# Sliding-window attention into a gated block on one core: two identity matrices built by VectorE from index tables, and three attention groups placed on other units

## The chip, the cores and the metric

The kernel runs on one core of a Trainium2 chip. The metric is the device time in microseconds (us) of one execution, taken as the median of several runs. A profile, taken by the hardware profiler in one further execution, gives the start and the length of each instruction on each engine. TensorE (PE in the profile) does the matmuls, with its weight loads shown apart as PEld; VectorE is DVE, ScalarE is ACT, GpSimd is POOL, and SyncE is SP. SP, ACT and POOL also issue the DMA transfers.

## The reference, cut to what matters

```python
# attention: batch 4, 8 heads, 768 positions, head size 64, 4 sink positions, window 128
scores = q @ k.T / 8
keep = (column < 4) | ((row - column >= 0) & (row - column < 128))
a = softmax(where(keep, scores, -1e9))
x = (a @ v), heads side by side      # 3072 tokens x 512
# gated block
g = x @ w_gate                       # 512 -> 1536
out = (g * sigmoid(g) * (x @ w_val)) @ w_out   # 1536 -> 512
```

Each query sees at most 128 keys behind it and the first four positions ("sinks").

## The kernel before, in words

**Groups and blocks.** The attention is cut into 12 groups of 256 tokens (three to a batch), each with two tiles `j` of 128 queries. The gated block is cut into eight token blocks (`SIZES`, line 43) of 256, 256, 256, 512, 512, 512, 512 and 256 tokens. The attention of later groups is woven by hand into the matmuls of the block, so that TensorE has work while the other engines do the softmax.

**The steps of a group `g`.** `T(g)` is two steps (line 533): each turns the keys and queries of half of the heads on TensorE with 64-wide matmuls against an identity (line 260) and has ACT and DVE copy them out (line 266); the second one also issues the loads of group `g+2` (`next_load`). Groups 0 to 3 take this way; groups 4 to 11 are turned by DMA transposes on SP (`C(g)`, line 304). `Ss(g)` is two steps of scores (line 333), each with four PSUM banks, an exponential per head on ACT (line 339) and a mask multiply on DVE (line 344). `K(g)` computes the scores against the sinks (lines 362 and 366). `PVs(g)` is four steps, one for each half of the heads `hh` and each tile `j`, in the order (0,0), (1,0) with the first half, then (0,1), (1,1) written as (j,hh): matmuls into one bank `o` (line 388), then on DVE a reciprocal (393) and a multiply into `xn` (400), which frees the bank. For group 3 and for groups 5 and up the second half of a tile ends with a DMA transpose of `xn` into `xT` on SP (line 406); the other groups turn `xn` on TensorE (`step_X`, 424).

**The block.** `gate` (436) projects a block of tokens: matmuls into `pg`, a tanh `th` on ACT (459), then any attention steps, then matmuls into `pv` (452), then on DVE `u` (466) and `ht` (467), which free `pg` and `pv`. `down` (494) multiplies the 12 pieces of `ht` with `w_out` (506), spreading its attention steps between them; ACT copies the result out (510) and SP writes it (512).

**Order.** Each engine runs its instructions in the order in which they were written. `weave` (556) walks a list of units (one `gate` or `down` call each), and `slots` says which attention steps are inside which unit. DVE work of a step is put into `later` and written out at the next `flush`: at the end of the unit's own products in a `gate`, after each step in a `down`. The first such list (652) has units 0 to 24; units 15 to 20 are the gates of block 2, unit 21 and 22 the downs of block 1, units 23 and 24 the downs of block 2. In the trace the `pg` matmuls of units 18, 19 and 20 start at 57.35, 59.47 and 61.58 us, and unit 21 at 64.49 us. After it comes block 3, which needs `xT` of groups 3 and 4. For block 5 (line 675) the units 0 to 11 are its gates.

**PSUM.** There are eight banks. A new tile takes the bank that comes free first in the written order, so the scores of a unit take the banks that older `o`, `pg` and `pv` tiles leave.

**The start.** DVE clears the identities `ident` and `id32`, the tile `wm` and others. TensorE runs eight matmuls on `wm` (245). POOL issues two loads of `kq` (167), then writes the diagonals of the two identities with an affine select each (`make_identity`), then two index tables `tq` and `tk` with iota (179 and 181), then the loads of `va`, of group 1, and of the weights. `build_masks` (217) has DVE compare `tq` and `tk` into the masks.

Of the kernel before, what the change touches and what calls it, by code (L numbers as in the profile page):

```python
# [7 lines left out]

FP32 = mybir.dt.float32
# [2 lines left out]
ALU = mybir.AluOpType  # L12
# [3 lines left out]
def kernel(  # L16
# [12 lines left out]
    nc = tc.nc  # L29
# [115 lines left out]
    ident = const.tile([P, P], BF16)  # L145
# [3 lines left out]
    tq = const.tile([P, P], FP32)  # L149
    tk = const.tile([P, 1], FP32)  # L150
# [4 lines left out]
        ks = const.tile([P, NP2 * KS], BF16, tag=f"ks{b}", name="ks")  # L155
        kss.append(ks)

    nc.vector.memset(ident, 0.0)
    wm = const.tile([P, 512], BF16)
    nc.vector.memset(wm, 0.0)  # L160
    wake = const.tile([P, 1], FP32)
# [10 lines left out]
            st[64:P], four_tokens(q, 0, slice(2 * p, 2 * p + 2)))  # L172
        first.append(st)
    id32 = const.tile([P, P], FP32)
    nc.vector.memset(id32, 0.0)
    make_identity(nc, ident, nomemset=True)
    make_identity(nc, id32, nomemset=True)

    nc.gpsimd.iota(tq, [[1, P]], base=0, channel_multiplier=0,
                   allow_small_or_imprecise_dtypes=True)  # L180
# [35 lines left out]

    def build_masks():

        tq2 = tq.rearrange("p (o x) -> p o x", o=1).broadcast_to([P, 2, P])
        nc.vector.tensor_scalar(mask[:, :, P:2 * P], tq2, tk, None, op0=ALU.is_ge)  # L220

        nc.vector.tensor_scalar(sk, tk, float(NS), None, op0=ALU.is_lt)
        flat, flat0 = (m.rearrange("p a x -> p (a x)") for m in (mask, mask0))
        nc.vector.tensor_scalar(mask[:, :, 0:P], tq2, tk, None, op0=ALU.is_lt)
        nc.vector.tensor_scalar(
            flat0[:, P:3 * P], flat[:, P:3 * P], sk, None, op0=ALU.max)
        nc.vector.tensor_copy(out=flat0[:, 3 * P:4 * P], in_=flat[:, 3 * P:4 * P])
# [5 lines left out]
    def A(fn, *a):  # L233
        return lambda: fn(*a)
# [35 lines left out]
    def step_T(g, ph, which=(0, 1), q_copy=None, q_late=False):  # L270

        if g not in kTs:
            new_kq(g)
        evict = turn(g, (2 * ph, 2 * ph + 1), which,
                     lambda i, p: nat[g][:, 2 * p:2 * p + 2], (ident, ident))
        if 0 in which:
            evict(0, nc.scalar.copy)
        if 1 in which:
            q = A(evict, 1, q_copy or nc.vector.tensor_copy)
            if q_late:  # L280
                later.append(q)
            else:
                q()
# [16 lines left out]
    def cross_T(g):  # L300

        t = crossp.tile([P, 2, 2, NP2, P], BF16, tag="kqT", name="kqT")
        for j in range(2):
            nc.sync.dma_start(
                t[:, j].rearrange("q i a m -> q (i a) m"),
                nat[g][:, j].rearrange("p i x -> p (i x)"), transpose=True)
        cross[g] = t
# [211 lines left out]
    def gates(tb):  # L519
        return [(gate, tb, f) for f in range(0, DFC, 512 // SIZES[tb])]  # L520

    def downs(tb):
        return [(down, tb, t) for t in range(SIZES[tb] // P)]

    def next_load(g):
        if g + 2 < NG:
            load1(g + 2)
            load_v(g + 2)

    def sinks(b):  # L530
        return [lambda: later.append(A(step_ks, b))]

    def T(g):
        def last():
            step_T(g, 1)
            next_load(g)
        return [A(step_T, g, 0), last]

    def Ss(g):
        return [A(step_S, g, p, p + 1) for p in (0, 2)]  # L540

    def PVs(g):

        return [A(step_PV, g, j, hh) for hh in range(2) for j in range(2)]

    def Xs(g):
        return [A(step_X, g, j) for j in range(2)]

    def K(g):
        return A(step_K, g)  # L550
# [5 lines left out]
    def weave(us, slots):  # L556
        assert all(i < len(us) for i in slots)
        for i, (fn, tb, x) in enumerate(us):
            fn(tb, x, slots.get(i, []))
# [7 lines left out]
    def slots(*pairs):  # L567
        sl = {}
        for at, steps in pairs:
            for i, step in zip(at if isinstance(at, tuple) else (at,) * len(steps),  # L570
                               steps):
                sl.setdefault(i, []).append(step)
        return sl

    def C(g):

        def last():
            cross_T(g)
            next_load(g)
        return [last]  # L580
# [4 lines left out]
    def first_T(p):  # L585
# [5 lines left out]
        evict(1, nc.vector.tensor_copy)  # L591

    build_masks()
    first_T(0)
    first_T(1)
# [47 lines left out]
    def first_PVs():  # L643
# [10 lines left out]
    weave(us, slots(  # L654
        (0, [flush, K(1), A(step_S, 1, 2, 3)]), (2, [first_PVs]),
        (3, [A(step_X, 1, 0), A(step_X, 1, 1, True), flush]),
        (9, T(2)), ((10, 11), Ss(2)), (10, [K(2)]),
        (12, PVs(2)[:2] + [flush]), (13, PVs(2)[2:] + [flush]), (13, C(4)),
        (14, [A(step_X, 2, 0), A(step_X, 2, 1, True), flush]),
        (15, T(3)), ((16, 17), Ss(3)), (17, sinks(1)), ((18, 18, 19, 19), PVs(3)), (19, [flush]),  # L660
        (18, C(5)), ((20, 21), Ss(4)), (21, [K(4)]),
        ((22, 22, 23, 23), PVs(4)), (24, Xs(4))))

    def pair(ga, gb, sh=0):
        s = sh
        return [((s, s + 2), Ss(ga)), ((s + 4, s + 5, s + 6, s + 7), PVs(ga)),
                ((s + 6, s + 8), Ss(gb)),
                ((10, 10, 11, 11) if s else (10, 11, 12, 13), PVs(gb))]
# [4 lines left out]
        (0, sinks(2)), *pair(7, 8), (3, [K(7)]),  # L673
        (4, C(9)), (11, C(10)), (14, C(11))))
    weave(gates(5) + downs(5), slots(
        (0, sinks(3)), *pair(9, 10), (6, [K(10)])))
    weave(gates(6) + gates(7) + downs(6) + downs(7), slots(
        ((0, 2), Ss(11)), ((4, 5, 6, 7), PVs(11))))

# [34 lines left out]
```

## Time and profile before

| what | value |
|---|---|
| median of 5 runs | 241.24 us (241.21, 242.59, 243.25, 241.24, 240.88) |
| the profiled execution | 241.21 us, its span 239.5 us |
| PE busy | 233.5 us, 98% of the span |
| DVE busy | 159.1 us, 66% |
| ACT busy | 113.2 us, 47% |
| POOL busy | 70.9 us, 30% |
| PE busy from 0 to 25 us | 22.42 of 25.00 |
| PE busy from 25 to 60 us | 35.00 of 35.00 |
| PE busy from 60 to 66 us | 5.78 of 6.00 |
| PE busy from 66 to 161 us | 95.00 of 95.00 |
| PE busy from 161 to 167 us | 5.83 of 6.00 |
| PE busy from 167 to 235 us | 68.00 of 68.00 |

The span is the time from the first to the last instruction of the profile; 1.7 us of the execution lie around it. "Busy" on PE includes time in which a matmul's pipeline drains, so a small wait of TensorE shows less in the busy time than in the distance between the starts of two groups of matmuls. The timeline of an engine has the start, the length, the operation and, in square brackets, the idle time before it with what ended it.

### The profile page before, as it was taken

The numbers are of one execution on the slowest core, as the hardware profiler recorded it, in microseconds if no ns is written. First come the engines' busy times: TensorE is split into PE (matmuls) and PEld (weight loads), VectorE is DVE, ScalarE is ACT, GpSimd is POOL, SyncE is SP. The second block draws the span as 40 slices with busy tenths as digits, with TensorE's granted clock in tenths as the row PEclk, the third lists the DMA queues.
The fourth block names the chain that finished last, engine by engine and source line by source line (L and its number), as shares of the span: only waits on it lengthen the run. The fifth ranks groups of instructions, "written<-read, shape, count | busy, mean of one in ns | idle before, by whom it ended". The sixth has DMA issues, their size and how long they took to land.

```text
span 239.5 us, 5227 instructions
## 1 busy us (share of the span) xinstructions
PE 233.5 (98%) x2083; PEld 135.8 (57%) x2083; DVE 159.1 (66%) x337; ACT 113.2 (47%) x230; POOL 70.9 (30%) x92
## 2 busy tenths in 40 slices
PE   7899999999999999999999999999999999999994
PEld 3578887678645445444445454444454445488444
DVE  4679788849963698970698961598971499877100
ACT  2888347248551764512755611556611662232112
POOL 8986387409817079000808000000000000000000
PEclk9999999999999999999999999999999999999999
DMA  7999999999999999918999936600204200200132
GB/s 140 162 183 197 204 190 204 167 208 116 151 165 164 213 162 143 114 22 206 128 154 85 146 67 170 127 0 4 44 0 131 90 0 3 44 0 3 45 131 88
DMA packets 98936, 27.37 MB, mean 114 GB/s; under 512 B 84832, under 2 KB 95968, under 8 KB 98912
## 3 DMA queue, kind: packets, MB, share of 16 engines
q0 software_dynamic: 68832, 13.90, 68.7%
q1 hardware_dynamic: 29504, 12.69, 24.8%
q10 hardware_dynamic: 576, 0.46, 0.6%
q8 instruction: 16, 0.26, 0.4%
q14 instruction: 8, 0.07, 0.1%
HBM read 28.34 MB, written 6.29 MB: 145 GB/s over the span
## 4 chain that ended last, share of the span: by engine, by line
PE 90%; ACT 4%; DVE 4%; issue 1%; DVEq 0%
PE pv L452 25%; PE pd L506 25%; PE pg L452 24%; PE o L388 5%; PE s L333 4%; ACT e L339 3%; PE pt L260 3%; PE wm L245 2%; DVE xn L400 1%; PE pd L487 1%; PE px L424 1%; DVE e L344 1%; ACT xn L396 1%; DVE u L466 1%; DVE rcp L393 0%
## 5 line engine op out<-in xcount | busy, mean ns | idle before, releaser
L452 PE MATMUL pv<-xT,wv 128*128 128x256 bf16 (+1 forms) x384 | 74.4, 326 | 0.3 <-DVE xn L400 0.3
L452 PE MATMUL pg<-xT,wg 128*128 128x256 bf16 (+1 forms) x384 | 74.2, 326 | 0.0
L459 ACT ACTIVATE th<-pg 128x512 f32<-128x512 f32 x72 | 43.8, 608 | 60.2 <-PE pg L452 59.7
L466 DVE SCALAR_TENSOR_TENSOR u<-th,pg 128x512 bf16<-128x512 f32 x72 | 49.1, 682 | 30.9 <-ACT th L459 30.2
L506 PE MATMUL pd<-wo,ht 128*128 128x512 bf16 x276 | 63.2, 379 | 0.0
L467 DVE TENSOR_TENSOR ht<-u,pv 128x512 bf16<-128x512 bf16 x72 | 49.5, 688 | 10.1 <-PE pv L452 3.2
L452 PEld LDWEIGHTS <-wg 128*128 128x128 bf16 x384 | 37.4, 98 | 25.4 <-issue 0.2
L339 ACT ACTIVATE e<-s 128x512 bf16<-128x512 f32 (+1 forms) x96 | 46.3, 581 | 1.6 <-PE s L333 1.3
L452 PEld LDWEIGHTS <-wv 128*128 128x128 bf16 x384 | 34.1, 98 | 20.6 <-issue 2.9
L506 PEld LDWEIGHTS <-ht 128*128 128x128 bf16 x276 | 26.0, 98 | 28.4 <-issue 0.2
L510 ACT ACTIVATE ot<-pd 128x512 f32<-128x512 f32 x23 | 13.7, 597 | 52.6 <-PE pd L506 50.2
L344 DVE TENSOR_TENSOR e<-e,mask 128x1024 bf16<-128x1024 bf16 (+2 forms) x49 | 29.1, 630 | 1.8 <-ACT e L339 1.7
L107 POOL DMA_DIRECT2D kq<-in_k_dram x16 | 14.4, 902 | 49.9 <-DMA kqT<-kq 49.1
L123 POOL DMA_DIRECT2D va<-in_v_dram x24 | 21.6, 920 | 2.1 <-DMA kq<-in_q_dram 0.7
L388 PEld LDWEIGHTS <-e 128*128 128x128 bf16 x352 | 16.3, 98 | 6.2 <-DVE e L344 0.9
L400 DVE TENSOR_TENSOR xn<-o,rcp 128x256 bf16<-128x256 f32 x44 | 18.7, 424 | 1.8 <-DMA xT<-xn 0.3
L388 PE MATMUL o<-va,e 128*128 128x65 bf16 x352 | 17.9, 193 | 0.3 <-DVE e L344 0.2
L107 POOL DMA_DIRECT2D kq<-in_q_dram x16 | 14.6, 911 | 1.1 <-DMA wo<-in_moe_w_out_dram 1.1
L393 DVE RECIPROCAL rcp<-o 128x4 f32<-128x4 f32 x48 | 8.3, 175 | 7.5 <-PE o L388 7.5
L491 DVE TENSOR_SCALAR ot<-pd 128x128 f32<-128x128 f32 x1 | 0.3, 292 | 14.4 <-PE pd L487 14.4
L333 PE MATMUL s<-kqT 64*128 64x128 bf16 (+1 forms) x168 | 9.4, 238 | 0.0
L388 PE MATMUL o<-vsb,es 128*128 128x260 bf16 x32 | 8.8, 274 | 0.0
(61 smaller groups left out, 107.5 us busy)
## 6 DMA issues: line engine op xcount, KB each, us to landing
out_dram<-ot SPq DMA_DIRECT2D x23, 256.0 KB
va<-in_v_dram POOLq DMA_DIRECT2D x24, 128.0 KB, 6.4
kq<-in_k_dram POOLq DMA_DIRECT2D x18, 128.0 KB, 4.4
kq<-in_q_dram POOLq DMA_DIRECT2D x16, 128.0 KB, 5.0
wo<-in_moe_w_out_dram POOLq DMA_DIRECT2D x4, 384.0 KB, 12.7
wg<-in_moe_w_gate_dram POOLq DMA_DIRECT2D x4, 256.0 KB, 8.0
wv<-in_moe_w_val_dram POOLq DMA_DIRECT2D x4, 256.0 KB, 8.5
kq<-in_k_dram POOLq DMA_DIRECT2D x3, 256.0 KB, 8.8
```

Source lines behind the costliest of these rows:

```text
L107: nc.gpsimd.dma_start(x[:, j, i].rearrange("p (h d) -> p h d", d=D), src[b, :, t0:t0 + P].rearrange("h m d -> m h d"))
L123: nc.gpsimd.dma_start(va[:, j, :, 0:D], v[b, :, t0:t0 + P].rearrange("h m d -> m h d"))
L333: nc.tensor.matmul(pss[2 * i + h][:, col:col + n * P], keys(b, t, r, p), queries(g, r, p, j, n), start=True, stop=True)
L339: nc.scalar.activation(e_t[g][:, 2 * p + h, lo:512], pss[2 * i + h][:, lo:512], AF.Exp, scale=scale)
L344: nc.vector.tensor_tensor(e, e, m[:, :, lo:512].broadcast_to([P, e.shape[1], 512 - lo]), op=ALU.mult)
L388: nc.tensor.matmul(o, l, r, start=(i == 0), stop=(i == len(mms) - 1), skip_group_check=True)
L400: nc.vector.tensor_tensor(xns[g, j][:, 256 * hh:256 * (hh + 1)].rearrange("p (h d) -> p h d", h=4), po[:, :, 0:D], rcp.broadcast_to([P, 4, ...
L452: nc.tensor.matmul(ps[:, i * n:(i + 1) * n], ws[fi][:, c, fo * P:(fo + 1) * P], x[:, 0:n // P, c], start=(c == 0), stop=(c == DMC - 1))
L459: nc.scalar.activation(th, pg, AF.Tanh, scale=0.5)
L466: nc.vector.scalar_tensor_tensor(u, th, 1.0, pg, op0=ALU.add, op1=ALU.mult)
L467: nc.vector.tensor_tensor(hts[tb][:, f:f + two].rearrange("p a n -> p (a n)"), u, pv, op=ALU.mult)
L506: nc.tensor.matmul(po, hts[tb][:, f, ts * P:(ts + 1) * P], wos[f // n][:, f % n], start=(f == 0), stop=(f == DFC - 1))
```

## The change

The two identities are no longer cleared by DVE and filled by POOL. DVE builds them in `build_masks`, ahead of the masks, by comparing the index tables for equality. POOL's affine selects are gone, so that its iota instructions and the loads behind them follow directly on the first two loads.

In the first list of units, the second `T(2)` step moves from unit 9 to unit 10, and `K(2)` from unit 10 to unit 11. The four `PVs(3)` steps, before two in unit 18 and two in unit 19 with a `flush`, are now one in each of the units 18, 19, 21 and 22. In block 5, `K(10)` moves from unit 6 to unit 5.

The line numbers in the text are those of the kernel before; in the changed kernel they are up to five lower.

```diff
-from concourse.masks import make_identity
...
-    nc.vector.memset(ident, 0.0)
...
-    nc.vector.memset(id32, 0.0)
-    make_identity(nc, ident, nomemset=True)
-    make_identity(nc, id32, nomemset=True)
...
     def build_masks():
+        for t in (ident, id32):
+            nc.vector.tensor_scalar(t, tq, tk, None, op0=ALU.is_equal)
         tq2 = tq.rearrange("p (o x) -> p o x", o=1).broadcast_to([P, 2, P])
...
-        (9, T(2)), ((10, 11), Ss(2)), (10, [K(2)]),
+        ((9, 10), T(2)), (11, [K(2)]), ((10, 11), Ss(2)),
...
-        (15, T(3)), ((16, 17), Ss(3)), (17, sinks(1)), ((18, 18, 19, 19), PVs(3)), (19, [flush]),
-        (18, C(5)), ((20, 21), Ss(4)), (21, [K(4)]),
+        (15, T(3)), ((16, 17), Ss(3)), (17, sinks(1)), ((18, 19), PVs(3)[:2]),
+        (18, C(5)), ((20, 21), Ss(4)), (21, [K(4)]), ((21, 22), PVs(3)[2:]),
...
-        (0, sinks(3)), *pair(9, 10), (6, [K(10)])))
+        (0, sinks(3)), *pair(9, 10), (5, [K(10)])))
```

## The prediction

> **What bounds the kernel now.** I read the page's busy times and chain first, then who waited for whom on PE, then the busy time by stretch, and last the timelines around the few places where PE waits.
>
> ```profile
> PE 233.5 (98%) x2083; PEld 135.8 (57%) x2083; DVE 159.1 (66%) x337; ACT 113.2 (47%) x230; POOL 70.9 (30%) x92
> PE 90%; ACT 4%; DVE 4%; issue 1%; DVEq 0%
> ```
>
> PE is the bound: nine tenths of the chain are its own work. Only PE's waits can be won, and they lie in three places, as the stretches in the table show: 0 to 25 us, around 63 us and around 164 us. Elsewhere PE is busy without a break.
>
> The second place, in the chain of waits:
>
> ```profile
> 60.50 0.14 PE o L388 x4
> ...
> 62.58 0.42 DVE xn L400
> ...
> 63.13 0.43 DVE xn L400
> ...
> 63.61 1.05 PE pv L452 x8
> ```
>
> Four `xn` multiplies of group 3 run one behind another on DVE (at 61.48, 62.03, 62.58 and 63.13), and PE's `pv` of unit 20 waits for the last. PE's timeline, here and at the third place:
>
> ```profile
> 61.58 1.04 PE L452 MATMUL pg<-xT,wg 128*128 128x256 bf16 x8
> 62.55 0.23 PE L333 MATMUL s<-kqT,kT 64*128 64x128 bf16 x2
> ...
> 63.61 1.05 PE L452 MATMUL pv<-xT,wv 128*128 128x256 bf16 x8 [0.16 <-DVE xn L400]
> ```
>
> ```profile
> 163.41 0.62 PE L333 MATMUL s<-kqT 64*128 64x128 bf16 x12
> 164.04 0.40 PE L362 MATMUL pk<-kqT,ks 128*32 128x256 bf16 x8
> 164.59 1.04 PE L452 MATMUL pv<-xT,wv 128*128 128x512 bf16 x4 [0.15 <-DVE xn L400]
> ```
>
> The twelve score matmuls from 62.55 to 63.61 take 1.06 us; the same twelve take 0.55 in unit 21 (65.45 to 66.00). The banks they ask for are those of group 3's `o` tiles.
>
> The start, on POOL and on DVE:
>
> ```profile
> 2.76 0.33 POOL masks.py:199 TENSOR_SCALAR_AFFINE_SELECT ident<-ident 128x128 bf16<-128x128 bf16 x1
> ...
> 3.26 0.27 POOL L179 IOTA tq<- 128x128 f32 x1
> 3.45 0.16 POOL L181 IOTA tk<- 128x1 f32 x1
> 3.53 1.84 POOL L123 DMA_DIRECT2D va<-in_v_dram  x2
> ```
>
> ```profile
> 3.64 0.35 DVE L220 TENSOR_SCALAR mask<-tq,tk 128x256 bf16<-128x256 f32 x1 [1.50 <-POOL tk L181]
> ...
> 4.80 0.58 DVE L227 COPY mask<-mask 128x128 bf16<-128x128 bf16 x1
> 6.18 0.42 DVE L266 CAST qT<-pt 128x256 bf16<-128x256 f32 x1 [0.80 <-PE pt L260]
> ```
>
> PE does not use the identities before its first transposes at 4.91 us, and these wait for the first `kq` load (the weight loads sat idle 0.89 us until it landed), not for POOL.
>
> **The change part by part.**
>
> *Group 3 spread.* In units 18 and 19 DVE now has one `xn` pair each in place of two. A pair (reciprocal and multiply) takes 0.55 us by the distance of the rows above. Following DVE's order: `ht` of unit 18 ends at 61.27 as before, the first pair at 61.82, `u` and `ht` of unit 19 at 63.2, the second pair at 63.75, `u` of unit 20 at 64.43. Units 18 and 19 had 24 `o` matmuls and now have 12, which is 0.36 us less work before unit 20 (twelve take 0.36, from 58.23 to 58.59), so PE wants the score banks from 62.55 − 0.36 = 62.2. They are now those of unit 17's `pv`, unit 18's `pg` and `pv`, and the first `o`: the last is free at 61.82. `pv` takes unit 19's `pg`, free after its `u` at 62.5, and is wanted at 62.75. No wait is left: 1.06 − 0.55 = **0.51 us** gained. The 0.36 of `o` matmuls come back in units 21 and 22. What is late next: the second scores of group 4 in unit 21 take the second `o` bank (free 63.75) and unit 20's `pg` (free 64.43), wanted at 64.3 and 64.5 (unit 21 starts at 64.49 − 0.51 − 0.36 = 63.62, its first three `pd` matmuls take 0.65, and the third bank is wanted 0.23 after the first). This fits by 0.07 only, so I charge 0.07 for it. Bounds of the part: 0.51, and 0, if the wait is only handed on to these two.
>
> *What the moved steps carry.* Each tile's second half ends in an SP transpose of `xn`. Before they were issued at 68.65, behind the two `kqT` transposes of group 5, which held SP from 64.69 to 68.54. Now the first `xn` is whole at about 68.2 (DVE has the group-4 masks first, 66.24 to 68.73 before, some 0.5 sooner now), so the first transpose still goes at about 68.65. The second stands behind the first (1.2 us) and unit 21's output (0.5 us): about 70.5 instead of 69.9. DVE's fourth `xn` of group 4's first half waited for the first transpose until 71.17 before, so one took 2.5 us to be read; the second would be in place by 73. Block 3 asks for it at 77.70 − 0.51 = 77.2. The cover is 4 us, so I cost it at nothing.
>
> *K(10) to unit 5.* From 163.41 to 164.59 PE takes 1.18 us for scores and `pk`. Scores take 0.55; four `pk` matmuls take 0.23 (37.60 to 37.83), so eight 0.45: 1.00 in all, and **0.18 us** are waits for DVE. With `pk` in unit 5, the `pv` of unit 6 takes the bank of unit 5's `pv`, whose `ht` ended at 163.99 before, and wants it at about 164.4 (163.41 + 0.45 + 0.55). The ACT exponential of `pk` moves from 165.79 into ACT's idle 1.37 us before 163.39. Bounds: 0.18 and 0.
>
> *Group 2 spread.* The same instructions, one unit apart. PE waits nowhere between 25 and 60 us, so nothing can be won. ACT's exponential of the sinks comes before the second scores' ones in unit 11 instead of after the first, which puts the last of those about 0.4 us later; their masks end about 43.5, and the PE step that needs them starts at 44.00. Cover 0.5 us: cost nothing. The loads of group 4 are issued at 37.88 behind others, after the moved transposes end (about 37.1), so they do not move. Bounds: 0, and −0.4 if that cover fails.
>
> *Identities.* DVE loses two clears (0.11 and 0.17 us) and gains two compares of 128 columns. None is in the trace: half of the 0.35 of the 256-column compare gives 0.18, the 0.58 of the 128-column copy is the other end. I take 0.2 each, nearest to the same operation. POOL drops 0.5 us (2.76 to 3.26), so `tk` is there at 3.1, the identities at 3.5, needed at 4.9. The masks end at 5.4 − 0.5 + 0.4 = 5.3, or 6.1 at the dear end; DVE's next work is at 6.18. Cost nothing either way.
>
> *Loads 0.5 us sooner.* In the PE rows above 25 us no wait ends in a weight or `va` load; the chain there runs over ACT exponentials, DVE and PE. From 16.57 on POOL itself waits for landings before it may issue (0.37, 0.59, 0.61 us and so on), so its lead turns into waiting. Value 0; bounds 0 and 0.5 gained. The first warm-up matmul may start 0.11 sooner, but the transposes behind it wait for the `kq` load: 0.
>
> [...]
>
> **The sum.** 0.51 + 0.18 less 0.07 for the tight place in unit 21 = 0.62. The profiled execution took 241.21 us, its span 239.5 and 1.7 around it; it stands 0.03 below the median. 241.21 − 0.62 = 240.6.
>
> **Rivals.**
>
> *The wait is handed on.* DVE is nearly full from 60 to 66 us (5.55 of 6.00) and no DVE work goes away, so the banks could be late elsewhere. Against it: DVE sat idle 0.76, 0.58, 1.19 and 0.57 us at 69 to 74, just where the moved pairs go. Time: 241.2 with nothing gained.
>
> *The loads count after all.* For it: gate weights land 7.3 to 10.6 us after issue, and the first, issued at 6.71, is used at 15.60, which leaves little. Then the full 0.5 comes on top: 241.21 − 0.51 − 0.18 − 0.5 = 240.0.
>
> *The late transpose of group 3 makes block 3 wait (slower).* If the second `xT` lands after 77.2, PE waits for each us beyond. Issued at 70.5 it decides from 6.7 us on. The nearest transpose took 2.5, but other transfers of this kernel took 5.0 (median of `kq`), 9.1 (`wv`) and up to 13.4. At 9.1 it would land at 79.6: 2.4 lost, 0.6 gained, 243.0.
>
> **How the numbers follow.** Forecast 0.60; handed on 0.18; loads 0.10; late transpose 0.07; the rest, a start that shifts by more than I see, 0.05. Low end: 240.0 less 0.3, which is how far the fastest run lies below the profiled one: 239.7. High end: nothing gained (241.2), 0.2 lost by the masks and 0.3 of scatter: 241.7. The late transpose stays outside. About 1% (2.4 us) is what a measurement of this kernel can tell from no change; the sum is a quarter of it. Faster by over 1% needs four times the sum: 0.04. Slower by over 1% needs a transpose later than 9 us or so: 0.06. Within 1%: 0.90.
>
> **What would show it.** Right: scores of unit 20 take 0.55 us; no `xn` in the chain around 63 us; `pv` follows `pk` at 162 without a wait; PE without idle time elsewhere after 25 us; the start before 25 us unchanged within 0.3 us although `va` is issued at about 3.0. Wrong: PE idle before block 3 at 77 us with `xT` as its releaser; identities over 0.6 us each; a new `xn` or `ht` wait in units 21 to 23; first transposes later than 5 us.

## The result

The changed kernel took 240.32 us (median of 41 runs, 239.73 to 241.97), the kernel before 241.06 us (78 runs): a ratio of 0.9967, 95% interval 0.9957 to 0.9977. That is 0.74 us less, by the interval 0.55 to 1.04. The forecast was 240.6 us, 0.62 under the profiled execution of the kernel before (241.21). The ratios, and the medians of the experiments, leave out executions far above the others of their kernel; the one in the profile of group 3 moved one unit too far is such a one (granted clock 0.986 in the mean), so its waits are read and its span is not.

The profiled execution of the changed kernel took 240.12 us, its span 238.4 us, 1.1 less than before. The page's busy times and the chain's shares by engine:

```profile
PE 232.8 (98%) x2083; PEld 135.5 (57%) x2083; DVE 159.1 (67%) x337; ACT 113.4 (48%) x230; POOL 70.4 (30%) x90
PE 91%; ACT 3%; DMA 2%; DVE 1%; issue 0%; POOL 0%; DVEq 0%; POOLq 0%
```

PE still bounds the kernel. DVE has the same work, POOL two instructions fewer, and a share of DMA has come into the chain, where there was none:

```profile
2.05 5.35 DMA kq<-in_k_dram
```

This is the second `kq` load of group 0. It is not among the loads that the change moves: both kernels issue it at 2.05 us, and it landed at 7.40 in place of 6.74. Over all 14 profiles it landed at 6.65 to 7.55 us (mean 7.17) in the six with early loads and at 6.74 to 7.12 (mean 6.89) in the eight others, so the loads issued sooner behind it may hold it up; no run tests that. Around 63 us the chain now reads (start, length, what):

```profile
60.90 0.87 PE pg L450 x8
61.78 0.55 PE s L331 x12
62.33 0.98 PE pv L450 x8
63.30 0.65 PE pd L504 x3
63.95 0.65 PE s L331 x12
```

No `o` and no `xn` stands between the pieces of PE any more. The twelve scores of unit 20 take 0.55 us in place of 1.06. Those of unit 21 take 0.65 in place of 0.55: the tight place that the prediction charged with 0.07. PE is busy for 6.00 of the 6.00 us from 60 to 66, and again from 161 to 167. The third place in PE's timeline:

```profile
162.96 0.62 PE L331 MATMUL s<-kqT 64*128 64x128 bf16 x12
163.51 1.04 PE L450 MATMUL pv<-xT,wv 128*128 128x512 bf16 x4
```

`pv` follows the scores after 0.55 us without a wait. The start, on POOL and on DVE:

```profile
2.76 0.28 POOL L174 IOTA tq<- 128x128 f32 x1
2.95 0.17 POOL L176 IOTA tk<- 128x1 f32 x1
3.03 1.91 POOL L122 DMA_DIRECT2D va<-in_v_dram  x2
```

```profile
3.16 0.29 DVE L216 TENSOR_SCALAR ident<-tq,tk 128x128 bf16<-128x128 f32 x1 [1.23 <-POOL tk L176]
3.36 0.65 DVE L216 TENSOR_SCALAR id<-tq,tk 128x128 f32<-128x128 f32 x1
...
4.70 0.30 DVE L225 COPY mask<-mask 128x128 bf16<-128x128 bf16 x1
5.85 0.89 DVE L264 CAST qT<-pt 128x256 bf16<-128x256 f32 x2 [0.84 <-PE pt L258]
```

The loads are issued 0.5 us sooner, and DVE is through with identities and masks at 5.0 us, long before its next work.

Where the 1.1 us of the span came from is read from the starts of groups of matmuls, which show waits that the busy time doesn't: PE's busy time from 60 to 66 us rose by 0.22, while the scores of unit 20 got 0.51 shorter. Each stretch lies between the first `pg` matmuls of two units or blocks, and the last one ends at the first `pd` of block 5's downs:

| stretch | before | after | difference |
|---|---|---|---|
| start to unit 0 | 15.60 | 15.00 | -0.60 |
| unit 0 to unit 9 | 17.62 | 17.62 | 0 |
| unit 9 to unit 12 (group 2) | 7.89 | 8.02 | +0.13 |
| unit 12 to unit 18 | 16.24 | 16.24 | 0 |
| unit 18 to block 3 (group 3) | 20.35 | 19.93 | -0.42 |
| block 3 to the downs of block 5 (K(10)) | 98.00 | 97.81 | -0.19 |

The three moved groups make -0.48 together, the start -0.60. That start is more than the forecast allowed (0.3), one of its signs of being right that did not come, so it is the main question of the experiments.

### The profile page after: what moved, and what is told of

Read it like the earlier page. It is cut to its first block, busy times and chain, and to the rows that moved or that the text cites. A ratio compares the mean times of both kernels' runs of the same rounds, so it can differ in the third digit from the quotient of the medians.

```text
span 238.4 us, 5224 instructions
## 1 busy us (share of the span) xinstructions
PE 232.8 (98%) x2083; PEld 135.5 (57%) x2083; DVE 159.1 (67%) x337; ACT 113.4 (48%) x230; POOL 70.4 (30%) x90
## 4 chain that ended last, share of the span: by engine, by line
PE 91%; ACT 3%; DMA 2%; DVE 1%; issue 0%; POOL 0%; DVEq 0%; POOLq 0%
PE pv L450 26%; PE pg L450 25%; PE pd L504 25%; PE o L386 5%; PE s L331 5%; DMA kq<-in_k_dram 2%; PE pt L258 2%; ACT e L337 2%; PE pd L485 1%; PE px L422 1%; DVE e L342 1%; ACT xn L394 1%; PE pk L360 1%; POOL kq L165 0%; ACT th L457 0%
```

## The experiments

Theory: the moved groups 3 and 10 give the gain, and the start of the profile taken after the change is not owed to the change. First rival: the earlier loads give a part of it. Second rival: the margin in front of block 3 is about to be used up. Ratios are to runs of the kernel before in the same job (a batch of runs on one chip), with 95% intervals; "start" is the first `pg` of unit 0 in the run's profile. A ratio on record is not just that of the two medians and lies up to 0.0025 off it: for "after, again" the medians give 0.9964. The kernel before has medians of 241.12, 240.99 and 241.16 us in the three jobs.

| kernel | median, us | ratio | start | 9 to 12 | 18 to block 3 | block 3 to downs 5 |
|---|---|---|---|---|---|---|
| identities alone | 240.88 | 1.0001 (0.9973 to 1.0029) | 15.03 | 7.94 | 20.15 | 97.99 |
| group 3 alone | 240.90 | 0.9982 (0.9962 to 1.0002) | 14.76 | 7.89 | 19.84 | 97.99 |
| K(10) alone | 240.86 | 0.9978 (0.9958 to 0.9998) | 14.81 | 8.10 | 20.21 | 97.80 |
| group 2 alone | 241.41 | 1.0021 (0.9995 to 1.0047) | 15.73 | 8.02 | 20.16 | 98.48 |
| before, again | 241.24 | 1.0007 (0.9989 to 1.0025) | 15.53 | 8.02 | 20.48 | 98.43 |
| after, group 2 back | 240.44 | 0.9977 (0.9960 to 0.9994) | 15.08 | 7.89 | 19.91 | 97.81 |
| after, loads 0.5 later | 240.57 | 0.9985 (0.9966 to 1.0004) | 15.46 | 8.02 | 20.03 | 97.81 |
| after, group 3 too late | 243.69 | 1.0116 (1.0084 to 1.0149) | 15.01 | 8.02 | 23.94 | not read |
| after, loads 1.5 later | 241.50 | 1.0004 (0.9976 to 1.0033) | 15.61 | 8.02 | 19.91 | 97.81 |
| groups alone | 240.83 | 0.9982 (0.9951 to 1.0012) | 14.74 | 8.57 | 20.04 | 97.80 |
| after, again | 240.29 | 0.9939 (0.9915 to 0.9964) | 15.56 | 8.02 | 19.84 | 97.80 |
| after, mended | 240.29 | 0.9945 (0.9924 to 0.9967) | 15.39 | 7.89 | 19.84 | 97.80 |

The first four and the next four rows are a job each, and the last four are one.

**One part alone.** Each kernel is the one before with one part of the diff shown above.

Identities:

> The kernel before with the identities built by VectorE and nothing else. If the start's 0.6 us in the profiled pair only came from the moment at which TensorE's matmuls become fast, this kernel equals the kernel before: 0.0 us (within 0.3), and its own profile may show either length of the first transposes. If the earlier loads or the shorter work of GpSimd bring it, it is 0.3 to 0.6 us faster, in this kernel's median too.

Group 3:

> The kernel before with only the four PV steps of group 3 spread over units 18, 19, 21 and 22. My theory: scores of unit 20 take 0.55 instead of 1.06 us, the scores of unit 21 lose 0.07 to 0.1, so 0.40 to 0.45 us faster. Rival (the wait is handed on): the chain shows DVE's xn or u in units 21 to 23 and the time is unchanged.

K(10):

> The kernel before with only K(10) moved from unit 6 to unit 5 of block 5. My theory: 0.18 us faster, with pv of unit 6 directly behind the scores. Rival: 0.0, the wait reappears one unit on.

Group 2:

> The kernel before with only the second T(2) step and K(2) one unit later. By the prediction 0.0 us. By the profile of the changed kernel 0.1 us slower, since two runs of 32 transposes take 0.57 us each where 64 in one run take 1.02.

Group 3 and K(10) shorten their own stretches and no other. Without K(10)'s move the last stretch takes 97.99 to 98.48, with it 97.80 or 97.81. Group 3's varies more: 20.15 to 20.48 without the move (five profiles, mean 20.27), 19.84 to 20.04 with it (eight, mean 19.92). The ratios point the same way; group 3's interval reaches 1 and K(10)'s just misses it. K(10)'s ratio would be 0.5 us, more than its stretch shows, so the sizes are taken from the stretches. Identities alone: not resolved. Group 2 alone did not come out at nothing: its stretch is 0.13 us longer than that of the kernel before. PE's timeline of the kernel before, and of the changed one, has the cause:

```profile
34.18 1.09 PE L260 MATMUL pt<-ident,kq 64*64 64x64 bf16 x64
35.20 1.05 PE L452 MATMUL pv<-xT,wv 128*128 128x256 bf16 x8
```

```profile
33.59 0.64 PE L258 MATMUL pt<-ident,kq 64*64 64x64 bf16 x32
34.16 1.05 PE L450 MATMUL pv<-xT,wv 128*128 128x256 bf16 x8
```

64 transposes in one run hold PE for 1.02 us (34.18 to 35.20), 32 for 0.57. Two runs of 32 are 1.14.

**The kernel before, once more, as a control.**

> The kernel before, unchanged, as a measure of the measurement: ratio 1.000 within its interval. Its profile shows where the transposes of the first two head pairs end. If TensorE's speed-up comes at a moment that the kernel does not set, this may differ by up to 1 us from the 6.99 us of the first profile; if the kernel sets it, it is 6.9 to 7.1 again.

The ratio's interval holds 1. In its profile the first scores start at 6.31 us, in the first profile of the same kernel at 6.92: the kernel does not set that moment.

**The changed kernel with group 2 as before.**

```diff
-        ((9, 10), T(2)), (11, [K(2)]), ((10, 11), Ss(2)),
+        (9, T(2)), ((10, 11), Ss(2)), (10, [K(2)]),
```

> The changed kernel with group 2 put back. If the split of the transposes costs 0.1 us, this is 0.1 faster than the changed kernel, about 0.85 faster than the kernel before; if group 2's spread helps, it is slower than the changed kernel.

Its stretch is back at 7.89. The 0.13 us don't show in the medians, which scatter by more.

**What sets the start.** In every profile TensorE's first transposes begin at 4.9 to 5.2 us. The timelines of PE at 5.8 us, of the kernel before and of the changed one:

```profile
5.89 0.31 PE L260 MATMUL pt<-ident,kq 64*64 64x64 bf16 x1
```

```profile
5.84 0.24 PE L258 MATMUL pt<-ident,kq 64*64 64x64 bf16 x1
```

The same matmul takes 0.31 us in the one and 0.24 in the other. Before, the transposes stay at 0.31 until the first scores at 6.92; after, they drop to 0.24 at 5.25, and the scores start at 6.32: 0.60 us sooner, which is the whole gain of the start. The granted clock reads 1.00 in both, so that row doesn't show it. It isn't the change either: with the identities as before (K(10) alone, group 3 alone) they are quick from 5.0 on, in four of six such profiles and in five of eight with the identities by DVE, and the changed kernel once more is slow until 6.4 and starts at 15.56:

> The changed kernel once more, as the measure for the other three. Ratio 0.997, 0.3 to 0.8 us under the kernel before. Its profile shows a first pg at 15.0 if TensorE gets quick before the first transposes end, and at about 15.5 if later: if the start of the profile taken after the change was owed to the change, 15.0 again; if it was owed to when TensorE gets quick, either.

That profile has the same start as that of the kernel before (15.56 and 15.60), and the two executions differ by 0.65 us (240.56 and 241.21), of which the stretches give 0.62: -0.51 (group 3), -0.20 (K(10)), +0.13 (group 2), -0.04 (start). Other matmuls change their pace too: the first ones on `wm` start 0.43 us apart, those of the same shape at 10.5 us in the kernel before 0.21 (the small transposes gain less, 0.31 to 0.24 in length). The moment moves: of the 14 profiles, nine have quick transposes from 4.9 to 5.7 us on, one of them (identities alone) quick matmuls from about 4.0, and five have quick ones only after 6.3, so it moves by more than 2 us. No run here shows what sets it. The seven earliest starts (14.74 to 15.08) all have quick transposes by 5.71 us, but that isn't enough: the control (15.53) and the mended kernel below (15.39) have them from 5.0 on and start late, since PE waited for loads (0.6 us in the one, 0.5 and 0.2 in the other).

**Do the loads count?** Here the changed kernel got two affine selects on tiles that nobody reads ahead of the index tables, with DVE's two clears, or six behind them:

```diff
+    nc.vector.memset(spare, 0.0)
+    nc.vector.memset(spare32, 0.0)
+    make_identity(nc, spare, nomemset=True)
+    make_identity(nc, spare32, nomemset=True)
```

> The changed kernel with GpSimd's two affine selects (and VectorE's two clears) put back on spare tiles that nobody reads, so that the loads are issued 0.5 us later, as before. If the earlier loads do nothing, the time is that of the changed kernel, 0.7 to 0.8 us under the kernel before. If they bring 0.3 or more, this is 0.3 slower than the changed kernel.

> The changed kernel with six more affine selects of POOL on tiles that nobody reads, behind the iotas, and two clears of these by DVE: the va loads and all behind them are issued about 1.5 us later than in the changed kernel, 1.0 later than in the kernel before. If the time of the loads doesn't matter up to there: within 0.2 us of the changed kernel in the same job, no PE wait on a DMA over 0.3 us before 26 us. If the loads bind when TensorE's start is quick: a PE wait on a DMA landing of 0.5 to 1.5 us before 26 us, and 0.5 to 1.0 us more than the changed kernel. If each 0.5 us is handed on in full: 1.5 us more, ratio about 1.003.

And the three groups alone, with the identities by GpSimd:

> The kernel before with groups 2, 3 and 10 moved, its identities as they were. If the identities and the earlier loads give nothing: the same time as the changed kernel, 0.46 us under the kernel before by the three sums from the profiles (0.40 and 0.19 gained, 0.13 lost), ratio 0.998. If they give something: 0.3 us or more above the changed kernel in the same job, ratio 0.999 or more. From the first pg of unit 9 to that of unit 12: 8.02 us; K(10) stretch 25.0; unit 18 to block 3 19.94.

In the last job the groups alone took 240.83 us and the changed kernel 240.29; eight of the twelve runs of the first lie above the slowest of the second (240.56). The difference of the medians is 0.54 us, by resampling the runs 0.13 to 1.32. With the loads 1.5 us later than in the changed kernel it is 1.21 us (0.76 to 1.94). So in this job the loads count, against the forecast. In the job before, the kernel with loads 0.5 us late stood 0.13 us (-0.25 to 0.33) over the one with group 2 back, and group 2 makes 0.13 of difference between these two by itself: there nothing is left for the loads. Identities alone, which has the loads 0.5 us sooner too, lay 0.25 us under the kernel before by the medians and level with it by the ratio. The loads' landings say that the lead lasts on the average: the second `kq` of group 2 landed at 32.97 to 33.64 us (mean 33.30) in the six profiles with early loads, at 33.07 to 34.22 (mean 33.77) in the seven with loads as before or put back to there. The two ranges overlap, so in a single pair of executions the lead can be gone.

The 1.21 us need not be the loads' alone. Beside POOL's six selects DVE took twice as long for the f32 identity (1.28 us in place of 0.65):

```profile
3.38 1.28 DVE L224 TENSOR_SCALAR id<-tq,tk 128x128 f32<-128x128 f32 x1
```

The masks ended at 6.38 in place of 5.0, and the first `qT` copy, which starts at 5.7 to 6.1 where the transposes are quick, had to stand behind them (6.32).

The profile of the groups alone shows how the loads get into the chain (its first part, in order of time):

```profile
2.76 0.32 POOL ident masks.py:199
3.08 0.24 POOL id masks.py:199
...
3.60 1.75 POOL va L123 x2
5.36 1.37 POOL kq L96 x2
...
10.23 9.55 DMA va<-in_v_dram
19.78 0.04 issue
19.82 0.39 PE o L388 x7
...
21.00 13.21 DMA kq<-in_q_dram
```

PE's start was early in this execution (14.74). So the chain runs not over PE, ACT and DVE, as before, but over POOL: the two affine selects, 0.56 us, stand in it, then all issues down to `va` of group 1, whose landing PE waits for, and on to `kq` of group 2. PE's list of waits:

```profile
PE o L388 <- DMA va<-in_v_dram: 0.6, 2, 0.4
PE pt L260 <- DMA kq<-in_q_dram: 0.3, 1, 0.3
```

From unit 0 to 9 this execution took 17.99 us, and from 9 to 12 8.57, in place of 17.62 and 8.02: 0.92 us lost, more than the early start had won. An early start with loads as late doesn't always pay so: group 3 alone started at 14.76 and lost nothing (17.63 and 7.89), its two `va` having landed 8.9 us after issue, by the median, and not 9.4. The changed kernel (15.00) kept its 17.62 and 8.02. The control lost in the same way: quick transposes, then 0.61 us of waiting at 13.5 us for the second `kq` of group 1. The profile with loads 1.5 us late started late itself (15.61) and shows no wait on a load over 0.3 us; that its median is 1.2 us worse is measured, but not how it divides between the loads and the late masks.

**The margin before block 3.** The second halves of group 3 one unit further on:

```diff
-        (18, C(5)), ((20, 21), Ss(4)), (21, [K(4)]), ((21, 22), PVs(3)[2:]),
+        (18, C(5)), ((20, 21), Ss(4)), (21, [K(4)]), ((22, 23), PVs(3)[2:]),
```

> The changed kernel with the second halves of group 3 one unit later still, in units 22 and 23. The second transpose to xT would then be issued at about 74 to 76 us instead of 72.5 and land 2.5 to 3 us later, and block 3 asks for it at 76.8. If the prediction's cover (4 us) were real nothing is lost; by the changed kernel's trace (the first transpose went 1.9 us later than predicted, the cover is some 2 us) 0.5 to 2 us are lost in front of block 3.

PE's timeline at the start of block 3:

```profile
76.56 1.03 PE L504 MATMUL pd<-wo,ht 128*128 128x512 bf16 x4
80.80 1.87 PE L450 MATMUL pg<-xT,wg 128*128 128x512 bf16 x4 [3.22 <-DMA xT<-xn]
82.46 1.91 PE L450 MATMUL pv<-xT,wv 128*128 128x512 bf16 x4
```

The rival that ended on the slower side is real one unit further on. The second `xT` was issued at 74.77 and let PE go at 80.80, 6.0 us later, and the matmuls behind the idle time ran at half their pace (1.66 us from start to start in place of 0.87). The granted clock, the third number from the end in this row of the busy times by stretch, was halved there:

```profile
80.80:82.50 1.70, 1.70 (x5) 0.60 (x6) 0.00 (x0) 0.00 (x0) 0.00 (x0) 0.50 2.21 191
```

The other five executions, with a granted clock of 0.993 to 1.00, still stand 3.1 us above the changed kernel with loads 0.5 us late (243.69 and 240.57), so the loss does not hang on that clock.

**A mended kernel.** The changed kernel with group 2 as before, and K(4) ahead of the second scores of group 4:

```diff
-        (18, C(5)), ((20, 21), Ss(4)), (21, [K(4)]), ((21, 22), PVs(3)[2:]),
+        (18, C(5)), (21, [K(4)]), ((20, 21), Ss(4)), ((21, 22), PVs(3)[2:]),
```

> The changed kernel with group 2 as before, and in unit 21 the sink scores K(4) written ahead of the second scores of group 4 in place of behind them. By the profiles group 2 costs 0.13 us and the scores of unit 21 wait 0.10: 0.2 us under the changed kernel, ratio 0.996. Unit 9 to unit 12: 7.89 us; scores of unit 21: 0.55 us for twelve. If the price of unit 21 only moves to the pk bank, 0.1 us under the changed kernel. If the moved exponential of the sinks delays the masks of group 4, a wait of PE for an o or xT in units 22 to 24 and no gain.

Both stretches have their shortest values (7.89 and 19.84), and unit 21's scores take 0.55 us. The start is a late one although the transposes were quick from 5.0 us on, since PE waited 0.5 us for the second `kq` of group 0 (landed at 7.55) and 0.2 for that of group 1: loads again. In time it can't be told from the changed kernel: 240.29 us each. The changed kernel's own second profile has 19.84 as well, so the 0.10 of unit 21 is not lost in every execution.

## Why the prediction was right, and where it was not

*Group 3 spread* (0.51, less 0.07). Right in mechanism, a little large in size: against the profile of before (20.35) it gives 0.51 in three profiles (19.84) and 0.31 to 0.44 in five, and 0.35 between the means with and without it. The 0.51 was read from one profile, and a stretch that waits is the one that varies. DVE's next work behind the first pair started at 61.53 (predicted 61.82) and behind the second at 63.47 (63.75), but unit 18 starts 0.47 us sooner in this profile (56.88 and 57.35), so against the matmuls both came 0.2 later than predicted. Unit 21's scores lost 0.10 us in the profile after, their third bank starting at 64.20, right behind the end of `u` of unit 20 (64.15), as the tight place said; in four others they lost nothing.

*K(10)* (0.18). Right: 0.19 or 0.20 against the profile of before in every profile that has it and was read.

*Group 2 spread* (nothing, or -0.4 if the masks' cover fails). Wrong by 0.13. The cover held, but "the same instructions, one unit apart" left out that two runs of transposes took 0.12 us more than one (1.14 and 1.02). With both halves in unit 9 the stretch took 8.02 and 8.10 in two other profiles (the control and K(10) alone), and there it was a load: the second transpose started 0.13 and 0.21 us after the first, at 34.26 and 33.62, right behind the landing of the second `kq` of group 2 (34.22 and 33.58). In the profiles with 7.89 that load had landed before the run of transposes began.

*What the moved steps carry* (cover 4 us). The conclusion held, PE waited for no `xT` with the change as it is, but the working did not. The prediction let the first transpose go at 68.65 as before. SP in the profile after:

```profile
66.56 3.92 SPq L302 DMA_TRANSPOSE kqT<-kq  x2
70.58 1.22 SPq L404 DMA_TRANSPOSE xT<-xn  x1
71.89 0.53 SPq L510 DMA_DIRECT2D out_dram<-ot  x1
72.52 1.22 SPq L404 DMA_TRANSPOSE xT<-xn  x1
```

The two `kqT` transposes ahead of it were issued 1.9 us later than before, because their `kq` landed later, and all on SP behind them moved along. The order on the queue was right, the time at its head was not: it hangs on a load. In the 14 profiles they are issued anywhere from 64.7 to 68.7 us. The second `xT` goes at 72.52 in place of 70.5 and, if it too takes the 2.6 us that DVE waited for the first one (70.58 to 73.18), is in place at 75.1, where block 3 starts at 76.8. The cover is 1.7 us by that, not 4, and the late case took 6.0. The chance of 0.07 was not too high.

*Identities* (nothing). As to DVE right: 0.29 and 0.65 us in place of 0.2 each, masks whole at 5.0, the first `qT` copy at 5.85 waits for PE. The 0.65 is over the 0.6 that was named as a sign of being wrong, for one identity of the two. The identity in f32 was slow by its row (0.65), the 128-column compare into bf16 was not (0.29); the next instruction started 0.20 us behind the start of either, and no loss came of it. The 0.2 us for the masks in the high end of the range is shown by no run: with the change as it is DVE was through with them at 5.0 and then idle for 0.84 us, until PE's first `pt`.

*Loads 0.5 us sooner* (value 0, bounds 0 and 0.5). This is the step that failed. It was read from one execution in which TensorE got quick late; there the start runs over PE, ACT and DVE, and the loads have slack. In an execution where TensorE is quick early the same loads can end last, as in the groups alone and the control. Nor does POOL's lead turn wholly into waiting: over the profiles the second `kq` of group 2 landed 0.47 us sooner on the average. The runs put the loads' share at 0.54 us (0.13 to 1.32) in one job and could not resolve it in others, so its size stays open. The rival, "the loads count after all", took the whole 0.5 on top and gave 240.0; the measured 240.32 lies between it and the sum.

So 240.6 came out near by luck in part, because terms were off in opposite ways: 0.13 lost by group 2 and about 0.1 less from group 3, against some tenths from the loads. One loss also comes without the change: in two profiles, the control and group 2 alone, PE lost 0.5 us at 106 us, behind an `ht` that stood behind an `xn` that waited 0.8 us for `xT`; that is why their last stretches are the longest.

## What to carry to other kernels

A term read as hidden in one profile is hidden only by the chain of that execution. Where two chains end within half a microsecond of each other at the start (here compute and loads), look at what the other would do if the first came sooner, before a load's time is put at nothing. For differences of a few tenths, compare distances between fixed matmuls, since the span holds a start that moves by itself (15.00 and 15.56 us in two profiles of one kernel here).

## What the runs showed of the hardware

- The 16 bf16 transposes ahead of the first scores took 0.31 us each in some executions and 0.24 in others, at the same granted clock of 1.00 on record. The first `pg` lay between 14.74 and 15.73 us, and one kernel had both 15.00 and 15.56.
- A 128-column compare on VectorE into f32 took 0.65 us by its row, and 1.28 with affine selects on GpSimd at the same time; into bf16 it took 0.29.
- Two runs of 32 transposes on TensorE took 1.14 us and one of 64 took 1.02, between the same other matmuls.
- A transpose by DMA on SP took 2.5 to 2.6 us until its source could be written again, and 6.0 until PE could go on in the late case.
- In one execution, idle time of 3.2 us on TensorE was followed by matmuls at half their pace (1.66 us from group to group in place of 0.87), at a granted clock of 0.50 on record.
